# Two gated matmul stages behind windowed attention: the sign bit of float64 weight words travels through ScalarE instead of VectorE

## The chip, the cores and the metric

The kernel runs on one core of a Trainium2 chip. The metric is the device time of one execution in microseconds, the median of several runs. The core has five engines with an instruction queue each, which run in order and meet only through semaphores: TensorE (PE, with its weight loads as PEld), VectorE (DVE), ScalarE (ACT), GpSimd (POOL) and SyncE (SP), which issues most of the DMAs.

## The reference

Attention over 4 batches, 8 heads, 576 positions and a head width of 64, with a causal window of 128 and a bias that falls with distance. Its output (2304 tokens of 512 values) goes through two dense stages:

```python
h = np.maximum(np.maximum(x @ w1, x @ w2), x @ w3)     # 512 -> 768
x = (h @ w_out).astype(np.float32)                     # 768 -> 512
g, val = x @ w_gate, x @ w_val                         # 512 -> 1536
out = (g / (1.0 + np.exp(-g)) * val) @ w_out           # 1536 -> 512
```

The weights arrive as float64, since they are float32 numbers that were multiplied by a float64 scalar. q, k, v are float32.

## The kernel before

Every matmul of float32 precision is made of three with operands of lower precision: an operand is kept as a head (its rounded value) and a rest (what rounding took away), and head times head, head times rest and rest times head are summed in PSUM.

The work is laid out as one program of pieces that are interleaved by hand. The attention is cut into units of up to 128 queries of one pair of heads; each unit passes through scores, normalising, transposes and values (`st_scores`, `st_normalise`, `st_transpose`, `st_values`). The first dense stage (`up_groups`, `down_groups`) runs between these units as soon as tokens are there, over six chunks of 384 tokens. The second dense stage (`second`) begins near 434 us in the profile; it uses seven products per block in place of eight, so it needs sums of weight blocks (`mixed`, line 582) and sums of token blocks (`token_sum`, line 646), and it walks over 12 blocks of hidden columns (`STEPS`). `spread` and the loop over `STEPS` say which piece is written behind which; the order that each engine then gets is chosen by a planner, which lays the instructions out in time by its own estimates of their costs and prefers the pieces under `high_priority`.

The change lies in `single` (lines 113 to 126), which turns float64 words into float32 in place. A weight tile lies in SBUF as pairs of 32-bit words, `lo` and `hi`. Line 118 (ACT) reads `hi` as a float32 and multiplies it by 2^-112, which takes 896 from the 11-bit exponent of the float64; the result goes into `w`, a tile of which there is one buffer (`wconv`). Line 121 (DVE) shifts `w` left by three bits, so that exponent and mantissa lie where a float32 has them; the sign, in bit 31, falls out. Line 122 (DVE) takes the sign from `hi` and puts it into `w`. Line 124 (DVE) shifts `lo` right by 29, which gives the last three mantissa bits, joins them with `w` and writes the finished float32 over `lo`.

`single` is called once for a tile by `prep_up` (9 tiles of 128 x 1024 for the first dense stage), `prep_down` (12 of 128 x 256), and `gates`, `values` and `outs` (36 of 128 x 512 for the second): 57 calls. What follows a call is `split`: line 129 (ACT) rounds the float32 to the head, and `low` (line 107, on DVE or POOL) subtracts to get the rest. The next call's line 118 can't write `w` before line 124 of the last call has read it.

Other lines that the prediction names: 359, 365 and 370 work on the scores (DVE, DVE, ACT's Exp); 380 and 387 are reciprocal and scaling on DVE; 398 is PE's transpose, 410 ACT's copy of its result; 201 is the maximum in the first dense stage; 621 loads token blocks (`yr`); 681 to 683 are PE's products in the second dense stage and 704 is ACT's copy of the first of them (`s`); 718 and 733 are Silu on ACT.

Of the kernel before, what the change touches and what calls it, by code (L numbers as in the profile page):

```python
# [8 lines left out]
F32 = mybir.dt.float32  # L9
# [3 lines left out]
AF = mybir.ActivationFunctionType  # L13
ALU = mybir.AluOpType
# [57 lines left out]
def kernel(ctx: ExitStack, tc, *args):  # L72
    n = len(NATIVE)
    qs, ks, qks = (dict(zip(u, x)) for u, x in ((NATIVE, args), (NATIVE, args[n:]), (ORDER[n:], args[2 * n:])))
    vv, w123, wo1, wgv, wo2, out = args[-6:]
# [10 lines left out]
    nc = tc.nc  # L86
# [26 lines left out]
    def single(raw, pinned=False):  # L113

        n = raw.shape[1]
        lo, hi = raw[:, :, 0], raw[:, :, 1]
        w = wconv.tile([P, 1024], I32, tag="wf", name="wf")[:, :n]
        first = nc.scalar.activation(out=w.bitcast(F32), in_=hi.bitcast(F32), func=AF.Copy, scale=2.0 ** -112)  # L118
        if pinned:
            tc.keep_in_program_order(first)  # L120
        nc.vector.tensor_scalar(out=w, in0=w, scalar1=3, scalar2=None, op0=ALU.logical_shift_left)
        nc.vector.scalar_tensor_tensor(out=w, in0=hi, scalar=-0x80000000, in1=w,
                                       op0=ALU.bitwise_and, op1=ALU.bitwise_or)
        nc.vector.scalar_tensor_tensor(out=lo, in0=lo, scalar=29, in1=w,  # L124
                                       op0=ALU.logical_shift_right, op1=ALU.bitwise_or)
        return lo.bitcast(F32)
# [5 lines left out]
    def prep_w(raw, t, pinned=False, rest=nc.vector):  # L132
        split(t, single(raw, pinned), rest)
# [118 lines left out]
    first = {}  # L252
# [300 lines left out]
    def second(apool, raws2, ps_o):  # L553
# [5 lines left out]
        def prep(f):  # L559
# [8 lines left out]
            def gates():  # L568
                ab[0] = single(raw[0])
                t[0] = up_tile(f"u{f}_0")  # L570
                split(t[0], ab[0], nc.vector)

            def values():
                ab[1] = single(raw[1])
                both = up_tile(f"u{f}_3") if f % 2 == 0 else ws[f - 1][5]
                t[3], t[5] = both[:, :, f % 2 * 256:f % 2 * 256 + 256], both
                split(t[3], ab[1][:, 256:], nc.vector)
# [368 lines left out]
```

## Time and profile before

| what | value |
|---|---|
| median of 3 runs | 849.52 us (849.43 to 849.52) |
| time of the profiled execution | 849.52 us |
| its span, first to last instruction | 847.8 us |
| granted clock of TensorE, mean of the span | 0.998 |
| PE busy | 834.7 us, 98% of the span |
| DVE busy | 599.0 us, 71% |
| ACT busy | 423.3 us, 50% |
| POOL busy | 382.9 us, 45% |

The span is the time from the first instruction of the program to the last one's end; the time of an execution holds 1.72 us more. Busy time of PE comes from matmuls that overlap, with modelled ends: a PE that is busy throughout may still be waiting a little between matmuls. In the views below, "idle" before an instruction is time in which its engine did nothing, and behind the arrow stands what ended the wait.

### The profile page before, as it was taken

The numbers are of one execution on the slowest core, as the hardware profiler recorded it, in microseconds if no ns is written. First come the engines' busy times: TensorE is split into PE (matmuls) and PEld (weight loads), VectorE is DVE, ScalarE is ACT, GpSimd is POOL, SyncE is SP. The second block draws the span as 40 slices with busy tenths as digits, with TensorE's granted clock in tenths as the row PEclk, the third lists the DMA queues.
The fourth block names the chain that finished last, engine by engine and source line by source line (L and its number), as shares of the span: only waits on it lengthen the run. The fifth ranks groups of instructions, "written<-read, shape, count | busy, mean of one in ns | idle before, by whom it ended". The sixth has DMA issues, their size and how long they took to land.

```text
span 847.8 us, 14703 instructions
## 1 busy us (share of the span) xinstructions
PE 834.7 (98%) x4760; PEld 781.0 (92%) x4760; DVE 599.0 (71%) x1593; ACT 423.3 (50%) x1146; POOL 382.9 (45%) x551
## 2 busy tenths in 40 slices
PE   8899999999999999999999999999999999999998
PEld 6589898999999999999999999999999999999996
DVE  8999798877666877549979999994753854343442
ACT  6776786776666677425356555553312422212220
POOL 2768898578877568635314232212311211211110
PEclk9999999999999999999999999999999999999999
DMA  9754443343232232314447498724947412827322
GB/s 328 250 168 147 123 130 112 122 137 95 81 113 92 65 117 62 108 37 147 145 163 281 162 342 300 250 87 145 352 148 262 147 65 77 299 98 253 106 75 99
DMA packets 62780, 133.34 MB, mean 157 GB/s; under 512 B 6768, under 2 KB 24176, under 8 KB 61552
## 3 DMA queue, kind: packets, MB, share of 16 engines
q1 hardware_dynamic: 59248, 127.69, 44.4%
q10 hardware_dynamic: 3456, 4.72, 1.6%
q8 instruction: 37, 0.61, 0.3%
q14 instruction: 39, 0.32, 0.1%
HBM read 96.99 MB, written 35.39 MB: 156 GB/s over the span
## 4 chain that ended last, share of the span: by engine, by line
PE 86%; DVE 7%; issue 2%; DMA 2%; POOL 1%; ACT 1%; SPq 0%; DVEq 0%; POOLq 0%; ACTq 0%
PE ps L157 9%; PE ps L156 9%; PE ps L158 9%; PE pg L682 7%; PE pg L681 7%; PE pg L683 7%; PE po L763 6%; PE po L762 6%; PE po L761 6%; PE pc L683 3%; PE pc L682 3%; PE pc L681 3%; PE pv L445 2%; PE sc L350 2%; PE pt L398 2%
## 5 line engine op out<-in xcount | busy, mean ns | idle before, releaser
L107 POOL TENSOR_TENSOR act<-h,act 128x384 fp32r<-128x384 f32 x72 | 79.6, 1126 | 287.4 <-ACT act L129 242.7
L157 PE MATMUL ps<-x,w 128*128 128x384 f32 x432 | 147.2, 341 | 0.0
L156 PE MATMUL ps<-x,w 128*128 128x384 f32 x432 | 146.0, 343 | 0.9 <-ACT m L199 0.9
L158 PE MATMUL ps<-x,w 128*128 128x384 f32 x432 | 146.3, 339 | 0.0
L681 PE MATMUL pg<-ya,u 128*128 128x384 f32 x360 | 120.4, 335 | 1.7 <-ACT s L704 1.7
L682 PE MATMUL pg<-ya,u 128*128 128x384 f32 x360 | 121.0, 336 | 0.0
L683 PE MATMUL pg<-ya,u 128*128 128x384 f32 x360 | 120.4, 335 | 0.0
L762 PE MATMUL po<-u,act 128*128 128x512 f32 x216 | 85.2, 394 | 0.0
L763 PE MATMUL po<-u,act 128*128 128x512 f32 x216 | 85.1, 395 | 0.0
L414 POOL TENSOR_SCALAR_AFFINE_SELECT t<-pk 128x512 fp32r<-128x512 f32 (+2 forms) x128 | 73.3, 595 | 24.2 <-DVE pk L107 16.1
L761 PE MATMUL po<-u,act 128*128 128x512 f32 x216 | 83.9, 389 | 0.0
L156 PEld LDWEIGHTS ps<-x,w 128*128 128x128 f32 x432 | 80.8, 188 | 2.7 <-ACT m L199 1.2
L690 DVE TENSOR_TENSOR u<-pg,s 128x384 f32<-128x384 f32 x72 | 39.7, 552 | 60.8 <-PE pg L683 60.6
L157 PEld LDWEIGHTS ps<-x,w 128*128 128x128 f32 x432 | 81.2, 188 | 1.3 <-issue 0.7
L158 PEld LDWEIGHTS ps<-x,w 128*128 128x128 f32 x432 | 81.2, 188 | 0.7 <-issue 0.7
L681 PEld LDWEIGHTS pg<-ya,u 128*128 128x128 f32 x360 | 67.6, 188 | 5.8 <-ACT s L704 2.0
L682 PEld LDWEIGHTS pg<-ya,u 128*128 128x128 f32 x360 | 67.6, 188 | 4.6
L370 ACT ACTIVATE z<-z,mn 128x128 f32<-128x128 f32 (+1 forms) x160 | 63.2, 398 | 10.5 <-DVE mn L365 10.1
L683 PEld LDWEIGHTS pg<-ya,u 128*128 128x128 f32 x360 | 67.6, 188 | 0.5
L718 ACT ACTIVATE h<-s 128x384 f32<-128x384 f32 x36 | 18.9, 524 | 90.7 <-DVE s L690 90.6
L118 ACT ACTIVATE wf<-wr 128x512 f32<-128x512 f32 (+2 forms) x57 | 39.8, 698 | 31.4 <-DVE wr L124 14.6
L690 DVE TENSOR_TENSOR u<-pc,u 128x384 f32<-128x384 f32 x72 | 39.8, 553 | 17.4 <-PE pc L683 17.1
(122 smaller groups left out, 2065.2 us busy)
## 6 DMA issues: line engine op xcount, KB each, us to landing
ya<-a_dram SPq DMA_DIRECT2D x56, 384.0 KB, 4.8
a_dram<-ya SPq DMA_DIRECT2D x42, 384.0 KB, 5.2
wr<-wgv SPq DMA_DIRECT2D x24, 512.0 KB, 4.5
wr<-w SPq DMA_DIRECT2D x9, 1024.0 KB, 5.5
qkr<-qk SPq DMA_DIRECT2D x32, 288.0 KB, 2.9
o_dram<-acc SPq DMA_DIRECT2D x36, 256.0 KB, 3.0
acc<-o_dram SPq DMA_DIRECT2D x36, 256.0 KB, 2.7
wr<-wo SPq DMA_DIRECT2D x12, 512.0 KB, 4.9
```

The costliest lines, as they stand in the source:

```text
L107: eng.tensor_tensor(out=out, in0=raw, in1=head.bitcast(F32), op=ALU.subtract)
L156: nc.tensor.matmul(ps, wh, xt_h, start=first, stop=False)
L157: nc.tensor.matmul(ps, wh, xt_l, start=False, stop=False)
L158: nc.tensor.matmul(ps, wl, xt_h, start=False, stop=last)
L414: nc.gpsimd.affine_select(out=t[:, i, :n, :, :m], in_=w[:, :n, :, :m], compare_op=op, fill=0.0, base=0, pattern=[[0, n], [0, 2], [-sign, m ...
L681: nc.tensor.matmul(o, wh, y[:, 0], start=first and k == 0, stop=False, skip_group_check=True)
L682: nc.tensor.matmul(o, wh, y[:, 1], start=False, stop=False, skip_group_check=True)
L683: nc.tensor.matmul(o, wl, y[:, 0], start=False, stop=k == 1, skip_group_check=True)
L690: nc.vector.tensor_tensor(out=o, in0=x, in1=y, op=ALU.add)
L761: nc.tensor.matmul(po, ah, w[:, 0], start=j == 0, stop=False)
L762: nc.tensor.matmul(po, ah, w[:, 1], start=False, stop=False)
L763: nc.tensor.matmul(po, al, w[:, 0], start=False, stop=j == PASS - 1)
```

## The change

Line 118 calls the parametric ReLU in place of Copy, with the same scale and a slope of 2^32 for negative inputs. A positive word is scaled as before. A negative one is multiplied by 2^32 as well, which adds 32 to its 8-bit exponent field and so sets bit 28, which is zero otherwise. Line 121 shifts by three, and bit 28 becomes bit 31, the sign. Line 122 is gone. Lines 121 and 124 stay as they were (124 becomes 122).

```diff
-        first = nc.scalar.activation(out=w.bitcast(F32), in_=hi.bitcast(F32), func=AF.Copy, scale=2.0 ** -112)
+        first = nc.scalar.activation(out=w.bitcast(F32), in_=hi.bitcast(F32), func=AF.Prelu, scale=2.0 ** -112, alpha=2.0 ** 32)
         if pinned:
             tc.keep_in_program_order(first)
         nc.vector.tensor_scalar(out=w, in0=w, scalar1=3, scalar2=None, op0=ALU.logical_shift_left)
-        nc.vector.scalar_tensor_tensor(out=w, in0=hi, scalar=-0x80000000, in1=w,
-                                       op0=ALU.bitwise_and, op1=ALU.bitwise_or)
         nc.vector.scalar_tensor_tensor(out=lo, in0=lo, scalar=29, in1=w,
                                        op0=ALU.logical_shift_right, op1=ALU.bitwise_or)
         return lo.bitcast(F32)
```

## Rows read from the trace of the kernel before

**Rows 1.** The page: busy time of each engine, share of the span, instructions.

```profile
PE 834.7 (98%) x4760; PEld 781.0 (92%) x4760; DVE 599.0 (71%) x1593; ACT 423.3 (50%) x1146; POOL 382.9 (45%) x551
```

**Rows 2.** Stretches: length, busy PE, PEld, DVE, ACT, POOL; clock, DMA share, GB/s.

```profile
0.00:20.00 20.00, 17.35 (x102) 12.75 (x102) 16.02 (x91) 12.29 (x44) 5.20 (x18) 1.00 0.90 326
20.00:40.00 20.00, 16.33 (x104) 11.84 (x100) 19.47 (x71) 14.84 (x50) 13.34 (x21) 0.91 0.73 245
...
100.00:120.00 20.00, 19.06 (x121) 18.12 (x120) 18.27 (x67) 16.87 (x55) 18.67 (x26) 1.00 0.47 145
...
420.00:440.00 20.00, 18.31 (x106) 17.99 (x105) 16.17 (x27) 9.76 (x18) 5.13 (x4) 1.00 0.67 234
...
500.00:520.00 20.00, 20.00 (x107) 18.73 (x106) 18.90 (x37) 11.36 (x25) 6.07 (x5) 1.00 0.81 279
840.00:848.00 8.00, 4.13 (x19) 3.08 (x17) 2.14 (x4) 0.00 (x0) 0.00 (x0) 1.00 0.51 189
```

**Rows 3.** PE's waits: for whom; us in total, times, the longest.

```profile
PE pg L681 <- ACT s L704: 1.7, 1, 1.7
PE pt L398 <- DVE z L387: 1.5, 1, 1.5
```

**Rows 4.** The removed instruction by form, on DVE, the form of 128 x 512.

```profile
L122 DVE SCALAR_TENSOR_TENSOR wf<-wr,wf 128x512 int32<-128x512 int32 x36 | 28.8, 799 | 0.4
```

**Rows 5.** Line 122 alone by stretch: length, busy DVE and count; clock, DMA, GB/s.

```profile
0.00:45.00 45.00, 4.89 (x4) 0.96 0.79 279
45.00:145.00 100.00, 14.20 (x17) 1.00 0.45 141
...
385.00:440.00 55.00, 6.70 (x9) 1.00 0.49 169
440.00:700.00 260.00, 21.39 (x26) 1.00 0.59 208
```

**Rows 6.** DVE in order of time near 25 us: start, duration, instruction.

```profile
23.52 1.24 DVE L122 SCALAR_TENSOR_TENSOR wf<-wr,wf 128x1024 int32<-128x1024 int32 x1
...
25.47 1.36 DVE L124 SCALAR_TENSOR_TENSOR wr<-wr,wf 128x1024 int32<-128x1024 int32 x1
...
26.83 0.35 DVE L387 TENSOR_SCALAR z<-z,rc 128x128 f32<-128x128 f32 x1
```

**Rows 7.** Stretches of 4 us near the first stalls, columns as in rows 2.

```profile
24.00:28.00 4.00, 2.27 (x24) 1.32 (x20) 4.00 (x16) 2.04 (x5) 2.46 (x4) 1.00 0.86 312
28.00:32.00 4.00, 4.00 (x23) 2.77 (x19) 4.00 (x13) 3.36 (x12) 2.00 (x3) 0.60 0.11 36
...
36.00:40.00 4.00, 2.98 (x21) 2.24 (x20) 3.98 (x15) 2.33 (x8) 3.35 (x5) 1.00 0.63 182
```

**Rows 8.** The chain that ended last, from 427 us: start, duration, what.

```profile
427.33 4.89 DMA yr<-y_dram
432.32 1.73 DVE yr L646
434.05 0.60 DVE wf L122
...
435.59 0.61 DVE wr L124
436.22 0.66 ACT u L129
436.89 0.38 ACT s L704
```

**Rows 9.** ACT by form: busy us, mean ns; idle before and its releaser.

```profile
L370 ACT ACTIVATE z<-z,mn 128x128 f32<-128x128 f32 x128 | 50.6, 398 | 9.1 <-DVE mn L365 8.9
L129 ACT CAST act<-h 128x384 fp32r<-128x384 f32 x72 | 33.5, 512 | 32.9 <-DVE h L693 32.9
...
L718 ACT ACTIVATE h<-s 128x384 f32<-128x384 f32 x36 | 18.9, 524 | 90.7 <-DVE s L690 90.6
...
L434 ACT CAST x<-pv 128x128 fp32r<-128x128 f32 x24 | 6.3, 261 | 6.7 <-PE pv L428 6.7
...
L733 ACT ACT_TABLE_LOAD x1 | 1.3, 1283 | 1.1 <-PE pg L683 1.1
```

## The prediction

> **What bounds the kernel now.** I read the busy times of the page first. PE is busy for 834.7 us of a span of 847.8 us [rows 1], so the whole kernel can gain 13.1 us at most by filling PE's idle time, whatever DVE is spared. The next question is where those 13.1 us lie, and the table of stretches answers it [rows 2]. At the end, from 840 us, 3.87 us are idle (8.00 less 4.13): the last addition and the last store, with no weight conversion near. The idle time that lies beside conversions is 2.65 us in the first 20 us, 3.67 us in the next 20, 0.94 us from 100 to 120, and 1.69 us from 420 to 440: 8.95 us together. In the stretch from 20 to 40 the granted clock is 0.91 as well, which is a loss of 0.09 x 20 = 1.8 us that the busy time hides. So 8.95 + 1.8 = 10.75 us is the most that the change can reach through PE.
>
> The third view is who ends PE's waits [rows 3]. Its longest wait, 1.7 us, is for ACT's copy at line 704 at the entry to the second dense stage; the next, 1.5 us, is for line 387 on DVE. DVE is 19.47 us of 20 busy from 20 to 40 us, 18.27 of 20 from 100 to 120 [rows 2]. There DVE is a second bound beside PE, and a shorter DVE queue can be worth something. From 500 to 520 us DVE is nearly as full (18.90 of 20), yet PE is busy for 20.00 of 20: there, what DVE is spared is worth nothing.
>
> **What is removed.** Line 122 costs 799 ns in its commonest form [rows 4], 57 of them in all. By stretch [rows 5]: 4 of them with 4.89 us in the first 45 us, 17 with 14.20 us up to 145 us, 9 with 6.70 us from 385 to 440, 26 with 21.39 us from 440 to 700; one more lies between. The 26 late ones, 45% of the sum, lie under a PE that has no idle time, so I cost their removal at nothing; what hides it is the products of the second dense stage. If that cover were gone (DVE late for PE), they would be worth up to 21.39 us, but no row there shows PE waiting.
>
> The first stall. At 23.52 us a line 122 takes 1.24 us on DVE; line 124 follows at 25.47 for 1.36 us, and behind it line 387 at 26.83 makes the operand of the transpose for which PE has been idle for 1.48 us (the 1.5 us wait) [rows 3, 6]. DVE has no gap in that stretch (4.00 of 4.00 busy [rows 7]). The removed 1.24 us stands in the same queue ahead of line 387, and another of its size stands some 8 us earlier (the four early ones average 4.89 / 4 = 1.22 us [rows 5]). Two of them are 2.46 us, more than the 1.48 us of the wait. So I take the wait as gone: 1.5 us. What is late next is ACT or POOL work of the neighbouring attention units; the bounds are 0 (another wait takes its place) and 3.67 us (all the idle time of the stretch).
>
> The clock behind it. In the 4 us with that stall PE is busy for 2.27 us, and in the next 4 us the granted clock is 0.60, a part of them at the lower level, 1.2 GHz in place of 2.4. From 36 to 40 us PE is busy for 2.98 us, and the rows show 1.00 there [rows 7]. With 1.48 us of the gap gone, the stretch from 24 to 28 would have 2.27 + 1.48 = 3.75 us busy, more than the one that kept its clock. So I take the fall of the clock as gone too: 0.40 x 4 = 1.6 us. Bounds: 0 and 1.8 us, and below nothing if a stall moves to where it brings the clock down once more (1.6 us lost).
>
> The entry to the second dense stage. The chain there goes from a load of a token block at 427.33 (4.89 us) through additions on DVE, a line 122 at 434.05 (0.60 us), line 124, ACT's line 129 and ACT's line 704, for which PE waits 1.7 us [rows 3, 8]. That load waits on SP for a weight buffer to come free, and the buffer comes free from DVE's work on the conversions. Of the 9 removed instructions between 385 and 440 us, 8 lie ahead of the load or in it and one behind it, at 0.6 to 0.8 us each [rows 4, 5, 8]; even three of them would cover 1.7 us. The loads of later weights on SP's queue come earlier by the same. I take 1.6 us of the 1.69 us that PE idles in the stretch [rows 2]. Bounds: 0 and 1.69.
>
> The stretch from 45 to 145 us holds the largest number of removed instructions (17) but little idle time, 0.94 us from 100 to 120 [rows 2]; a load lies ahead of that gap as well. I take 0.3 us; bounds 0 and 0.94.
>
> **What is added.** Line 118 changes its function, not its size. No row shows a parametric ReLU. The nearest one is Silu over 128 x 384 at 524 ns against 512 ns for a cast of the same shape: 12 ns more [rows 9]. The far one is Exp, with a bias read from SBUF and a sum, over 128 x 128 at 398 ns against 261 ns for a cast: 137 ns more [rows 9]. I take the near one, since scale and slope are plain numbers as they are for Silu: 57 x 12 ns = 0.7 us, spread over ACT, which is half idle [rows 1]. The far end is 57 x 137 ns = 7.8 us of ACT, some 21/57 of it (2.9 us) in the stretch where attention waits for ACT too; a tenth of that reaching PE would be 0.3 us. In the sum it is nothing. The Trainium skill, page "ScalarE: Activation LUTs", section "What ACT_TABLE_LOAD costs", adds about 93 ns for each operand that an ACTIVATE reads by pointer; by it the estimate would be 57 x 93 ns = 5.3 us of ACT at most, and the row for Silu, 524 ns, shows no such addition.
>
> What else moves: no DMA is added. No wait is added: line 121 waits for line 118 as before, and line 124 now follows it directly. The next line 118 gets the one `w` buffer earlier. The planner, however, lays out every queue anew with 57 instructions fewer, and this is the cost that no row gives. I take 0, and as its bounds one stall like the first, with its clock, to either side: 1.5 + 1.6 = 3.1 us.
>
> **The sum.** 1.5 + 1.6 + 1.6 + 0.3 = 5.0 us. The profiled execution took 849.52 us, 1.72 us more than its span, and is itself the median of the runs shown. 849.5 - 5.0 = 844.5 us.
>
> **The rivals.** First: only the entry to the second stage gains, because the early stalls belong to the attention's own chain of ACT, POOL and DVE, which is late by another link when one is shortened. For it: several of PE's early waits are ended by ACT and POOL. Against it: DVE without a gap. Time: 849.5 - 1.7 = 847.8 us, on the border of what can be told from no change (0.2% is 1.7 us, about what a measurement of this kernel can tell; below I use that bound).
>
> Second: nothing is gained, because the planner fills the room with earlier conversions, and the load at 427 us waits for something else: 849.5 us.
>
> Third, the other side: conversions move forward in ACT's queue. In the first 45 us ACT works on line 118 and line 129 in turn with the Exp and the copies that feed transposes; both work on 128 x 1024. If the planner, with a shorter DVE part per conversion, puts line 129 of a conversion ahead of such a copy and it must wait there for line 124, the copy waits with it. It decides from the point where that wait is longer than PE's queued work; then one more stall with its clock comes, 3.1 us, and nothing is regained: 852.6 us. For it: ACT is only 14.84 us of 20 busy there and waits in order. Against it: line 124 now comes sooner.
>
> Fourth, a table: ACT might have to load a table for the new function between Exp and Silu. The trace has a load before Silu, 1283 ns [rows 9]. 21 conversions lie among Exp in the first 145 us, with two loads each 21 x 2 x 1.283 = 54 us. ACT's three early rows average 14.7 us of 20 [rows 2], so some 145 x 0.267 = 39 us are free, and 15 us at least go over: 865 us or more. The Trainium skill, page "ScalarE: Activation LUTs", section "Table sets: the hidden batching unit", says that cheap functions such as relu and copy stand in every set; it doesn't name the parametric one there, and no run here shows it. One load serves Exp and Copy in this trace, which speaks for cheap functions being shared.
>
> **How the numbers follow.** My forecast, a gain of 3 to 8 us: 0.50. A larger gain, up to the bound of 10.75 us: 0.05. First rival 0.17, half of it beyond the border (0.09) and half within (0.08). Second 0.11. Third 0.13. Fourth 0.04. So faster 0.50 + 0.05 + 0.09 = 0.64, same 0.08 + 0.11 = 0.19, slower 0.17. The range goes from 840.0 (the forecast and nearly all of the larger gain) to 851.5 (the two rivals near no change and the nearer third of the third): about 0.15 is left out, the fourth, most of the third and a little of the large gains.
>
> **What would show it.** Right: PE's idle time from 20 to 40 us falls from 3.67 us to near 2, the clock row near 28 us reads 1.00, PE's wait for line 704 is gone, the last 8 us are as before, DVE's busy time falls by about 48 us, and line 118 keeps its duration within 20 ns. Wrong: the clock falls elsewhere in the first 45 us; the wait at the entry to the second stage stands with a load as its releaser; more table loads than now; or PE's waits on ACT's copies grow.

## The result and the profile after

The changed kernel takes 853.1 us (852.67 to 858.31, 6 runs), the kernel before 849.61 us (849.43 to 849.91, 6 runs) beside it. The ratio of the times, after over before, is 1.0051 with a 95% interval of 1.0028 to 1.0074: it is slower by 0.5% (0.4% by the medians; one run of after took 858.31 us, at a mean granted clock of 0.992). The forecast was 844.5 us and its range ended at 851.5, so it was wrong in sign and in range. The profiled execution of after took 853.82 us, with a span of 852.1 and a mean granted clock of 0.996. Behind the old line 122 all line numbers of after are smaller by two (704 is 702, 129 is 127, 124 is 122).

The page, busy time of each engine, to be read beside [rows 1]:

```profile
PE 836.6 (98%) x4760; PEld 781.8 (92%) x4760; DVE 556.9 (65%) x1536; ACT 423.7 (50%) x1146; POOL 364.6 (43%) x551
```

DVE lost its 57 instructions and 42.1 us. ACT is as busy as before. PE has two microseconds more busy time, and the table of stretches tells where from; the columns are those of [rows 2].

```profile
0.00:20.00 20.00, 17.04 (x98) 12.63 (x98) 15.56 (x89) 12.27 (x40) 5.88 (x18) 1.00 0.91 327
20.00:40.00 20.00, 16.78 (x110) 12.02 (x109) 19.14 (x73) 16.72 (x57) 12.66 (x21) 1.00 0.84 284
100.00:120.00 20.00, 19.38 (x119) 17.39 (x118) 16.27 (x62) 15.46 (x53) 17.85 (x28) 1.00 0.35 108
420.00:440.00 20.00, 19.78 (x113) 19.14 (x112) 7.59 (x11) 8.29 (x15) 6.31 (x5) 1.00 0.27 86
440.00:460.00 20.00, 18.77 (x105) 18.00 (x105) 15.41 (x28) 10.78 (x23) 6.82 (x6) 1.00 0.77 285
460.00:480.00 20.00, 16.68 (x86) 15.55 (x85) 18.37 (x36) 9.78 (x21) 4.82 (x4) 0.91 0.60 190
480.00:500.00 20.00, 20.00 (x96) 18.41 (x95) 12.30 (x22) 9.27 (x20) 7.01 (x6) 0.92 0.65 236
```

Idle time of PE is 20 less its busy time, and (1 - clock) x 20 is the PE time that the lower clock takes. In these seven stretches:

| stretch, us | idle before | idle after | clock before | clock after |
|---|---|---|---|---|
| 0 to 20 | 2.65 | 2.96 | 0 | 0 |
| 20 to 40 | 3.67 | 3.22 | 1.8 | 0 |
| 100 to 120 | 0.94 | 0.62 | 0 | 0 |
| 420 to 440 | 1.69 | 0.22 | 0 | 0 |
| 440 to 460 | 0 | 1.23 | 0 | 0 |
| 460 to 480 | 0 | 3.32 | 0 | 1.8 |
| 480 to 500 | 0 | 0 | 0 | 1.6 |
| sum | 8.95 | 11.57 | 1.8 | 3.4 |

The sums are 10.75 before (the 8.95 + 1.8 of the prediction) and 14.97 after. Their difference of 4.2 us is close to the 4.3 us by which the span grew (852.1 - 847.8). The three stretches up to 120 us gave 2.3 us back (1.8 of it the clock), the one from 420 to 440 us gave 1.5, and the second dense stage from 440 us, where PE had been busy throughout, took away 7.95. PE's waits by their enders (us in total, times, longest) name the large one:

```profile
PE po L759 <- ACT act L127: 3.3, 1, 3.3
PE pt L396 <- ACT pk L408: 1.6, 3, 1.2
...
PE pg L679 <- ACT s L702: 1.2, 1, 1.2
```

The 1.7 us for the first copies by line 704 of [rows 3], at the entry to the second stage, are gone. The 1.2 us for line 702 are a new wait, for a later copy, and it ends at 445.89 us. ACT in order of time ahead of that copy (start, duration, and in brackets the idle time before and its ender):

```profile
438.53 0.49 ACT L731 ACTIVATE h<-pg 128x384 f32<-128x384 f32 x1
444.26 0.66 ACT L118 ACTIVATE wf<-wr 128x512 f32<-128x512 f32 x1 [5.24 <-DMA wr<-wo]
444.82 0.51 ACT L716 ACTIVATE h<-s 128x384 f32<-128x384 f32 x1
445.36 0.48 ACT L702 COPY s<-pg 128x384 f32<-128x384 f32 x1
```

A line 118 stood still for 5.24 us, until its block of down weights (`wo`) had landed, and the Silu and the copy behind it in the queue waited with it. The 3.3 us for `act` are new as well. ACT around them, in the same columns:

```profile
471.41 0.93 ACT L127 CAST ya<-yr 128x384 fp32r<-128x384 f32 x2 [0.85 <-DMA yr<-y_dram]
476.62 0.66 ACT L118 ACTIVATE wf<-wr 128x512 f32<-128x512 f32 x1 [4.28 <-DMA wr<-wo]
477.18 0.91 ACT L127 CAST act<-h 128x384 fp32r<-128x384 f32 x2
```

And the chain that ended last, over the same time:

```profile
470.06 6.54 DMA wr<-wo
476.60 0.02 issue
476.62 0.03 ACT wf L118
476.65 0.53 issue
477.18 0.51 ACT act L127
477.69 0.04 issue
477.73 0.80 PE po L759
```

Here too ACT stood still, for 4.28 us, at a line 118 whose block of down weights was still under way, and behind it in the same queue stood the two casts whose result PE needed. The clock fell to its lower level, 1.2 GHz, at 476.5 us, in that gap, and stayed there for 6.8 us: half of that, 3.4 us, is the clock's column of the table. In four of the other five runs of after the mean clock was 0.997 or 0.998, so they lost less to the clock than the profiled one (0.996).

In the order of ACT's queue this line 118 stands directly ahead of those casts. In the kernel before the same line 118 stands behind six instructions that it precedes here: both casts, two Silu and two copies. There it waits for its load too:

```profile
484.56 0.67 ACT L118 ACTIVATE wf<-wr 128x512 f32<-128x512 f32 x1 [2.80 <-DMA wr<-wo]
```

That load was issued at 479.19 us, 9 us later than the 470.06 us of after, and yet PE was busy for 20.00 of 20 us from 480 to 500 us. So it is not a later load that makes the stall of after; what is new is the work that stands behind the wait.

### The profile page after: what moved, and what is told of

Read it like the earlier page. It is cut to its first block, busy times and chain, and to the rows that moved or that the text cites. A ratio compares the mean times of both kernels' runs of the same rounds, so it can differ in the third digit from the quotient of the medians.

```text
span 852.1 us, 14597 instructions
## 1 busy us (share of the span) xinstructions
PE 836.6 (98%) x4760; PEld 781.8 (92%) x4760; DVE 556.9 (65%) x1536; ACT 423.7 (50%) x1146; POOL 364.6 (43%) x551
## 5 line engine op out<-in xcount | busy, mean ns | idle before, releaser
L107 POOL TENSOR_TENSOR act<-h,act 128x384 fp32r<-128x384 f32 x72 | 77.6, 1099 | 293.8 <-ACT act L127 237.5
L118 ACT ACTIVATE wf<-wr 128x512 f32<-128x512 f32 (+2 forms) x57 | 39.7, 696 | 32.0 <-DMA wr<-wo 23.7
L702 ACT COPY s<-pg 128x384 f32<-128x384 f32 x36 | 17.3, 480 | 75.9 <-PE pg L681 75.8
```

The source lines that it names most:

```text
L107: eng.tensor_tensor(out=out, in0=raw, in1=head.bitcast(F32), op=ALU.subtract)
```

## The experiments

Ratios below are time over the time of the kernel before on the same chip (849.9 to 850.2 us), with 95% intervals. Differences in us between two kernels that ran beside different measurements of the kernel before hold up to 0.6 us of theirs (849.61 to 850.24). The theory that arose from the profile is that the removal itself gains and the planner's new order loses, in the second stage through the place of that one line 118. The rivals are that the new function costs something, that the loss belongs to the removal in any order, that the load is what is late, and that the stall matters less than the clock early in the kernel.

**The function alone.** Line 118 with the parametric ReLU, line 122 kept; every queue has the order of before.

```diff
-        first = nc.scalar.activation(..., func=AF.Copy, scale=2.0 ** -112)
+        first = nc.scalar.activation(..., func=AF.Prelu, scale=2.0 ** -112, alpha=2.0 ** 32)
...
         nc.vector.scalar_tensor_tensor(out=w, in0=hi, scalar=-0x80000000, in1=w,
                                        op0=ALU.bitwise_and, op1=ALU.bitwise_or)
```

> Line 118 calls the parametric ReLU as in the changed kernel, but line 122 of the kernel before stays (it sets a sign that is set already), and every engine's queue has the order of the kernel before. Theory (the loss is one of order, the function costs nothing): 849.6 us, within 0.5, line 118 at 670 ns within 5, two table loads of 1283 ns. Rival (the function itself costs): some 0.14 us for each of 57, 850.5 to 853 us, and line 118 longer.

It took 849.9 us, ratio 1.0002 (0.9993 to 1.0011). ACT by form in after (busy us, mean ns of one, idle before), the new function at 128 x 512 and both table loads:

```profile
L118 ACT ACTIVATE wf<-wr 128x512 f32<-128x512 f32 x36 | 24.1, 669 | 23.9 <-DMA wr<-wo 15.8 <-DVE wr L122 4.3 <-DMA wr<-wgv 3.3
...
L368 ACT ACT_TABLE_LOAD x1 | 1.3, 1283 | 0.8 <-PEq L933 0.8
L731 ACT ACT_TABLE_LOAD x1 | 1.3, 1283 | 0.0
```

Copy took 671 ns at this shape in the kernel before, which had two table loads of 1283 ns as well. The new function costs nothing.

**The removal alone.** The code of after, with each engine held to the order that it had before, less line 122. A recorded list per engine gives the order, and neighbours in it are tied without a wait:

```diff
         tile_attention_moe_moe_kernel(tc, *args)
+        keep_orders(nc, tc)   # per engine: for a, b in zip(order, order[1:]):
+                              #   tc.add_manual_dep(mine[b], mine[a].name, DependencyInfo(NoSync, DATA))
```

> The changed kernel, but each queue is held in the order that it has in the kernel before, with line 122 left out. Theory (the removal itself is worth what the forecast's sum said, and the new order takes it away): 844.5 to 846 us, PE's wait of 1.5 us near 27 us and its wait of 1.7 us near 435 us gone. Rival (PE is the bound everywhere and the removal is worth nothing): 849.5 us. Rival (without line 122 something in the second stage is late whatever the order): 852 us or more.

It took 846.68 us (845.04 to 847.28, 5 runs, all with a clock of 1.000), ratio 0.9954 (0.9942 to 0.9966). Stretches, and PE's waits, of this kernel, in its fastest run:

```profile
0.00:20.00 20.00, 16.60 (x96) 12.26 (x97) 14.78 (x89) 11.54 (x44) 6.22 (x18) 1.00 0.92 323
20.00:40.00 20.00, 16.88 (x114) 12.12 (x112) 16.99 (x70) 16.19 (x54) 11.36 (x21) 1.00 0.77 262
...
420.00:440.00 20.00, 19.32 (x112) 19.00 (x111) 12.32 (x21) 9.49 (x18) 3.17 (x2) 1.00 0.47 155
440.00:460.00 20.00, 20.00 (x114) 19.61 (x113) 18.49 (x33) 12.89 (x28) 8.43 (x7) 1.00 0.82 296
460.00:480.00 20.00, 20.00 (x108) 18.82 (x107) 19.12 (x34) 11.00 (x23) 4.57 (x5) 1.00 0.49 153
```

```profile
PE pt L396 <- ACT pk L408: 2.2, 5, 1.0
PE pv L426 <- POOL t L412: 1.6, 4, 0.9
...
PE pg L679 <- ACT s L702: 0.7, 1, 0.7
```

The removal gains 3.3 us (849.99 - 846.68), and the second stage keeps its cover: 20.00 of 20. So the loss is the order's: 853.1 - 846.7 = 6.4 us. The waits also show where it stayed below the forecast's 5.0. The clock from 20 to 40 us is 1.00, as forecast, and the entry wait fell from 1.7 to 0.7. But the first stall didn't vanish: PE now waits for ACT's copies (line 408) and POOL's selections (line 412).

**The order alone.** Line 122 kept, directly behind line 121, with all else in the order of after.

```diff
         nc.vector.tensor_scalar(out=w, in0=w, scalar1=3, scalar2=None, op0=ALU.logical_shift_left)
+        nc.vector.scalar_tensor_tensor(out=w, in0=hi, scalar=-0x80000000, in1=w,
+                                       op0=ALU.bitwise_and, op1=ALU.bitwise_or)
```

> The kernel before, with line 122 in place, but each queue is held in the order that it has in the changed kernel (line 122 directly behind its line 121). Theory (the order is what costs): 853 us or more, with PE's long wait near 474 us for ACT's line 129 and a fall of the clock behind it; up to some 6 us more than the changed kernel, since the early stalls are back. Rival (the removal is what costs): near 849.5 us.

It took 877.19 us, ratio 1.0316 (1.0302 to 1.0329). PE's waits:

```profile
PE po L761 <- ACT act L129: 5.6, 2, 5.2
PE ps L156 <- DVE m L201: 4.4, 3, 1.6
PE pv L428 <- POOL t L414: 3.5, 6, 1.7
```

The same wait for `act` heads the list, now with 5.2 us at once. Up to some 6 us more than after had been expected. The loss isn't in one place: PE's idle time is larger than in after by 4.3 us up to 45 us, by 5.7 from 45 to 145, by 4.2 from 385 to 440 and by 4.1 from 440 to 520. With this order line 122 is worth 877.2 - 853.1 = 24 us, in the order of before 3.3 us. The two parts of the change are not a sum: an order laid out for a DVE without line 122 is far worse with it than the old order was. What an instruction is worth depends on the order into which it is put.

**One instruction moved.** The orders of after, except that the stalled line 118 goes two places back in ACT's queue, behind the two casts.

```diff
-    ACT: [..., 118 of wo, 127 act<-h, 127 act<-h, ...]
+    ACT: [..., 127 act<-h, 127 act<-h, 118 of wo, ...]
```

> The changed kernel in its own orders, but for one instruction: the line 118 of the conversion that waits at 476.6 us for its weights stands two places later in ACT's queue, behind the two casts for which PE waits 3.3 us. Theory (this one place makes the wait and the fall of the clock): the 3.3 us wait and some 3.4 us at half clock are gone, 846 to 847.5 us. Rival (DVE, which also waits there for line 118, makes PE wait in the same place): a wait of 2 us or more near 476 us stays, 850 to 853 us. Rival (the late load only moves its wait to the next copy on ACT): 849 to 851 us.

It took 849.8 us (847.19 to 853.14, 12 runs), ratio 0.9996 (0.9983 to 1.001), 3.3 us less than after. ACT in order of time:

```profile
473.40 0.93 ACT L127 CAST act<-h 128x384 fp32r<-128x384 f32 x2 [1.44 <-DVE h L691]
476.68 0.68 ACT L118 ACTIVATE wf<-wr 128x512 f32<-128x512 f32 x1 [2.35 <-DMA wr<-wo]
```

The load lands at the same time as in after, so line 118 starts at the same time (476.68 us against 476.62), and the casts are done 3.8 us earlier. PE's gap there fell from 3.3 to 0.1 us, as the theory had it, but the time stayed above its 846 to 847.5 us. The runs spread more than the stall explains: those with a mean clock of 0.999 or 1.000 took 847.2 to 849.3 us, those with 0.995 to 0.998 took 850.3 to 853.1.

**The whole conversion moved.** The same conversion moved further: its line 118 six places back, its lines 121 and 122 on DVE seven places back.

```diff
-    ACT: [..., 118 of wo, <6 others>, ...]    DVE: [..., 121, 122 of wo, <7 others>, ...]
+    ACT: [..., <6 others>, 118 of wo, ...]    DVE: [..., <7 others>, 121, 122 of wo, ...]
```

> The changed kernel in its own orders, but for the three instructions of that one conversion: line 118 goes six places back on ACT (to where it stands in the kernel before, behind two casts, two Silu and two copies), lines 121 and 122 go seven places back on DVE, behind the additions that had queued behind them. Theory (the early place in both queues is what costs, and what is left when only ACT's is mended is DVE's part and the landing of the load): 846.5 to 848 us, with the single runs within 2 us of one another. Rival (another place of the new order loses as much, whatever is done here): 849 to 851 us and as wide as when one was moved.

It took 850.67 us (846.32 to 852.09, 12 runs), ratio 0.9998 (0.9985 to 1.0011). Moving it further gains nothing more, and the spread stayed: 4 runs at a mean clock of 0.999 or 1.000 took 846.3 to 848.4 us, 8 at 0.996 took 850.4 to 852.1. So the spread is not this conversion's, and the runs were not within 2 us of one another as the theory had it. It follows the clock, which falls in some runs and not in others; the two halves of the order, further below, put most of that into the early part.

**The planner, told to leave them.** `single` can keep line 118 in written order; here for the down weights of the second stage, with the planner laying out the rest anew.

```diff
-                ab[2] = single(raw[2])
+                ab[2] = single(raw[2], pinned=True)
```

> The changed kernel, planned anew with one instruction held: line 118 of a conversion of down weights may not stand on ACT ahead of what is written before it. Theory (the planner puts it forward because it takes the load as landed): PE's wait of 3.3 us for line 127's casts is gone, no fall of the clock near 476 us, 846 to 849 us. Rival (the plan finds another stall of the size): 850 to 853 us.

It took 849.17 us (844.96 to 851.0), ratio 0.9976 (0.9963 to 0.999). In its profile the longest wait of PE between 400 and 840 us is 0.19 us. The three runs with a clock of 1.000 took 845.0 to 846.5 us, the two with 0.998 took 848.4 and 849.0, the seven with 0.995 or 0.996 took 849.2 to 851.0; in the profiled one the clock fell at 23.7 us, for 3.4 us. The second stage is whole; the start is not.

**An earlier load.** The loads of the first four blocks of down weights written one conversion earlier, planned anew: if the load is what is late, this mends it.

```diff
-                return out + [piece for pieces in todo for piece in pieces[4:]]
+                loads, outs = [pieces[4] for pieces in todo], [pieces[5] for pieces in todo]
+                return out + loads[:1] + [piece for n in range(len(todo)) for piece in loads[n + 1:n + 2] + outs[n:n + 1]]
```

> The changed kernel, planned anew, with the load of each of the first four down weights written one conversion earlier. Theory (the load that lands late is what ACT waits for): the wait on ACT for that load falls from 4.3 us to near 0, 846 to 849 us. Rival (the load waits on SP for one of five buffers, so that writing it earlier only holds up the loads behind it): 851 us or more.

It took 851.3 us (848.39 to 856.23), ratio 1.0017 (1.0001 to 1.0032). PE's wait for `act`, and the load ahead of it in the chain:

```profile
PE po L760 <- ACT act L127: 1.5, 1, 1.5
```

```profile
471.18 4.91 DMA wr<-wo
```

Line 118 still waits 21.0 us in 11 waits for `wr<-wo` (23.7 us in 11 in after). Written earlier, the load was not issued earlier: 471.18 us against 470.06 in after. So the outcome is the rival's, and what a load that is really earlier would be worth, this run doesn't show. The place of line 118 can be mended in the order of ACT, the load's time could not be in this way.

**A sliver of line 122.** After, with line 122 on 8 of its columns, so that the planner lays out a third order.

```diff
+        nc.vector.scalar_tensor_tensor(out=w[:, :8], in0=hi[:, :8], scalar=-0x80000000, in1=w[:, :8],
+                                       op0=ALU.bitwise_and, op1=ALU.bitwise_or)
```

> The changed kernel with line 122 of the kernel before kept on 8 columns only (it sets a sign that is set already): some 57 x 0.1 us on DVE in place of 47.9 us. Planned anew. Theory (each plan finds its own stalls, and the time of one says little of the next): off the changed kernel's 853.1 us by 2 us or more, to either side, from 844 to 858 us, with stalls in other places. Rival (the time follows the work on DVE): within 1 us of the changed kernel, 852 to 854 us.

It took 849.49 us (847.88 to 852.59), ratio 0.9993 (0.9981 to 1.0004): with 57 instructions more than after it is 3.6 us faster. Its largest stalls lie elsewhere (near 21, 26, 129 and 439 us); the longest:

```profile
PE pg L681 <- ACT h L733: 1.5, 1, 1.5
```

Between after and this kernel the time doesn't follow DVE's work, it follows the order.

**The two halves of the order.** The order of before up to some 365 us and that of after behind it, and the reverse.

```diff
-    order of after, whole
+    e9_old_head: before's order to 365 us, after's order behind
+    e10_old_tail: after's order to 365 us, before's order behind
```

> The changed kernel with each queue held to the order of the kernel before up to some 365 us (line 122 left out), and to its own order behind that. Theory (the second stage's order is most of the loss): 849.5 to 852 us, the wait of 3.3 us near 474 us and the fall of the clock behind it as in the changed kernel, and the early stretch as when the removal stands alone. Rival (the early order is the loss): 846 to 847.5 us.

> The other half: the changed kernel's own order up to some 365 us, the order of the kernel before behind that. Theory (the early order costs nothing in the mean): 846 to 847.5 us, the clock whole. Rival (the new early order has a stall of 1.4 us near 21 us, behind which the clock falls in part of the runs): 848 to 850.5 us, with single runs in two groups some 3.4 us apart by their mean clock (1.000 and 0.996).

With the old head it took 852.82 us (851.58 to 853.44), ratio 1.0033 (1.0021 to 1.0045). The wait for `act` and the two stretches around it:

```profile
PE po L759 <- ACT act L127: 4.3, 1, 4.3
```

```profile
460.00:480.00 20.00, 15.72 (x81) 14.68 (x80) 17.40 (x34) 8.81 (x19) 4.81 (x4) 0.94 0.58 183
480.00:500.00 20.00, 20.00 (x102) 18.44 (x101) 12.62 (x22) 9.28 (x20) 7.05 (x6) 0.97 0.69 252
```

With the old tail it took 848.77 us (846.57 to 854.23, 12 runs), ratio 0.9987 (0.9973 to 1.0001), in two groups: six runs with a clock of 0.999 or 1.000 at 846.6 to 847.6 us, six with 0.993 to 0.996 at 849.9 to 854.2; that is the rival's outcome. Against the removal alone, the new order behind 365 us costs 852.8 - 846.7 = 6.1 us by the medians, with its five runs within 1.9 us of one another, and the new order ahead of it 848.8 - 846.7 = 2.1 us, which is about nothing in the six runs whose clock held. The profiled run of the old tail, 854.23 us, shows where it doesn't:

```profile
20.00:24.00 4.00, 2.45 (x14) 1.33 (x12) 3.98 (x10) 3.35 (x14) 1.98 (x2) 1.00 0.95 305
24.00:28.00 4.00, 3.60 (x15) 2.44 (x16) 2.02 (x12) 3.05 (x7) 1.42 (x4) 0.51 0.91 325
```

The same two stretches in the profiled run of after, which has that order at this place:

```profile
20.00:24.00 4.00, 2.07 (x12) 1.03 (x12) 3.99 (x17) 3.35 (x14) 2.00 (x4) 1.00 0.80 243
24.00:28.00 4.00, 3.77 (x26) 2.80 (x26) 3.22 (x10) 3.38 (x12) 0.90 (x3) 1.00 0.99 306
```

PE was idle for longer in after (1.93 us of 4 against 1.55), yet kept its clock; in the old tail it didn't. Not all of the 854.23 us is the early order's: the clock of this run fell once more, from 440 to 460 us (0.91, 1.8 us), behind a wait of 2.0 us at the entry to the second stage, in the old order.

**One place, against the old head.** The old head as above, with the one line 118 two places back.

```diff
-    ACT: [..., 118 of wo, 127 act<-h, 127 act<-h, ...]
+    ACT: [..., 127 act<-h, 127 act<-h, 118 of wo, ...]
```

> As the kernel with the old head (old order up to some 365 us, the changed kernel's own behind that; 852.82 us), but for the one line 118 that goes two places back on ACT, behind the two casts. The early stretch, which makes the clock differ from run to run in the new early order, is out of it. Theory (that one place is all that the second stage loses): 846.5 to 848 us, the wait of some 4 us near 474 us below 0.5, no fall of the clock behind it. Rival (the rest of the new second-stage order loses as well): 849 to 851 us.

It took 847.93 us (846.4 to 849.53, 8 runs, all with a clock of 0.999 or 1.000), ratio 0.9976 (0.9965 to 0.9986).

```profile
460.00:480.00 20.00, 19.34 (x103) 17.68 (x102) 17.35 (x34) 9.58 (x21) 4.68 (x4) 1.00 0.58 184
480.00:500.00 20.00, 20.00 (x103) 18.15 (x103) 14.93 (x28) 11.55 (x26) 6.54 (x5) 1.00 0.80 285
```

852.82 - 847.93 = 4.9 us for one instruction in one queue, two places from where it was. The stretches say about the same: PE's idle time there falls from 4.28 to 0.66 us (3.6), and the clock's loss from (0.06 + 0.03) x 20 = 1.8 us to nothing, 5.4 us together; the profiled run, 849.53 us, is the slowest of the eight, and its span is only 3.5 us shorter. What is left in the second stage is the other wait seen in after: 1.0 us of PE for line 702, behind a line 118 that waits 5.03 us for its load.

**The version that beats both.** The order of before up to some 365 us, and behind it the order that the planner gave with the pinned conversions.

```diff
-    order of after, whole
+    before's order to 365 us, the pinned kernel's order behind
```

> The order of the kernel before up to some 365 us, and behind that the order that the planner gave with line 118 of the down weights held in the written order; line 122 is out. The best of both as far as known. Theory (the early stretch then keeps its clock and the second stage has no stall over 0.4 us): 845 to 846.5 us, faster than the removal alone by some 0.5 us. Rival (the stalls seen with the pin come from the stretch near 464 us and take the clock): 847.5 to 849.5 us.

It took 845.09 us (844.82 to 845.78, 5 runs), ratio 0.9946 (0.9934 to 0.9958), at a clock of 0.999 or 1.000 in every run. Both waits behind a line 118 are gone:

```profile
440.00:460.00 20.00, 20.00 (x113) 19.48 (x112) 18.79 (x30) 12.65 (x28) 8.02 (x7) 1.00 0.64 236
460.00:480.00 20.00, 19.83 (x105) 18.26 (x104) 19.93 (x37) 11.55 (x24) 6.94 (x6) 1.00 0.68 239
```

It is the fastest measured, though its interval overlaps that of the removal alone.

## Why the prediction was wrong

**The step that failed** is the sentence on the planner: "I take 0, and as its bounds one stall like the first, with its clock, to either side: 1.5 + 1.6 = 3.1 us." It measured 6.4 us on the bad side, twice the bound. 6.1 us were measured for the new order behind 365 us alone, and 4.9 of these hang on the place of one instruction. The term was sized by the first stall, one of those in the trace of before. A new order can put a stall where the old one had none, and there it was larger: 3.3 us in after and 4.3 in the old head's, with a clock fall that took 3.4 and 1.8 us in these profiled runs.

**"The 26 late ones ... I cost their removal at nothing"** was right for the removal: held to the old order, PE stays busy for 20.00 of 20 from 440 to 480 us. But the working then asked only whether DVE could be late for PE there. It was ACT's queue in its new order that took the cover away. That nothing in a covered stretch can gain doesn't mean that nothing in it can lose.

**The third rival** had the mechanism: a conversion moves forward in ACT's queue and holds up work behind it. Its price of 852.6 us is near the 853.1 by luck: it is one early stall of 3.1 us with nothing regained, and the runs show 3.3 us regained and 6.4 lost. Its place was wrong, the first 45 us for the second stage, and so was what is waited for, line 124 for a load. It got a chance of 0.13. The rows for a better one were at hand: line 118 already waited for loads of weights in the trace of before (8.1 us for `wr<-wo` in 6 waits), in a queue that holds the casts for PE.

**The terms of the sum.** The first wait, 1.5 us: mis-sized. The wait for line 387 went, and ACT's copies and POOL's selections came in its place, as the bound of 0 had it. In the removal alone the idle time from 20 to 40 us fell by 0.55 us (3.67 to 3.12), and that from 0 to 20 rose by 0.75 (2.65 to 3.40). The entry, 1.6 us: 1.0 in the removal alone (1.69 to 0.68). The stretch from 100 to 120 us, 0.3 us: right (0.94 to 0.64).

The clock near 28 us, 1.6 us: right that the fall goes, 1.00 in after's profile and in the removal alone. But the reasoning behind it (a stretch busier than that of [rows 7] from 36 us keeps its clock) was too sure, since gaps of nearly the same size near 21 us bring the clock down in some runs only. And its price is in doubt. Beside the experiments the kernel before ran 87 times: 43 runs had a mean clock of 0.999 or 1.000 and a median of 850.1 us, and 39 had 0.997 or 0.998, as the profiled one had, and a median of 849.9. In that kernel a run that kept its clock was no faster. In the two profiles the four stretches of the prediction give the removal 1.1 us of idle time and 1.8 us of clock; the 87 runs say that the 1.8 can't be taken as a gain by itself. No trace shows a run of the kernel before that kept its clock, so how the 3.3 us divide stays open.

**The function** was right at nothing: 669 ns against 671 of Copy, and two table loads as before. The fourth rival is out. The Trainium skill, page "ScalarE: Activation LUTs", section "Table sets: the hidden batching unit", left open whether the parametric form stands in every set; here it shares Exp's and Silu's. By the price for operands in the section "What ACT_TABLE_LOAD costs" of that page, quoted in the prediction, which is one for an operand read by pointer, 57 instructions would have cost an estimated 5.3 us of ACT; the rows show none of it for a scale and slope given as plain numbers.

**The signs that were named.** Line 118 kept its duration within 20 ns: seen. DVE's busy time fell by 42.1 us, not 48: other instructions of DVE grew by the rest. The idle time from 20 to 40 us fell to 3.22 us, not to 2. The clock near 28 us reads 1.00: seen. The last 8 us are as before: seen, PE busy for 4.33 us against 4.13. The wait for line 704 at the entry is gone: seen, but a new one of 1.2 us ends some 9 us further on, and its releaser stood behind a line 118 that waited for a load. Of the signs for wrong, "PE's waits on ACT's copies grow" is the one that came: from 1.0 to 1.6 us for line 408 (410 before), and from nothing to 3.3 us for the casts of `act`.

**What stays open.** Why a gap near 21 us takes the clock in one run and not in the next. What a load that is issued earlier would be worth. Why the load at 470.06 took 6.54 us, when loads of this kind take 4.7 us in the median of the page: SP issued five stores right behind it, which may have shared the DMA engines with it, but no run varied that. And why the planner chose that place; its own estimates of time are in no trace.

## What to carry to other kernels

Where a planner or scheduler lays out the queues, an edit has two prices, its work and the new order, and the second can be the larger: measure the edit once with the old order held, and only then with the new one. In an in-order queue look for instructions that wait for a DMA and ask which work stands behind them; put such an instruction behind the casts that TensorE needs, or pin it. A stretch with a full TensorE promises no gain, but it must stand in the list of what can be lost.

## What the runs showed of the hardware

The clock was seen to fall to its lower level for 3.4 us (the old head, near 478 us) or 6.8 us (after, from 476.5 us), behind gaps of PE. The mean clock of one and the same kernel differed from run to run: the old tail had 0.999 or 1.000 in six of twelve runs, and its median then depends on how often the clock falls, 846.6 to 847.6 us against 849.9 to 854.2. That isn't so in every kernel: in the kernel before, runs with 0.999 or 1.000 and runs with 0.997 or 0.998 took the same (850.1 and 849.9 us). An in-order queue passes on a wait for a DMA: 5.24 us of ACT behind one line 118 became 1.2 us of PE, 4.28 us behind another 3.3 us. The parametric ReLU, with scale and slope as plain numbers, costs on ACT what Copy costs (669 and 671 ns at 128 x 512), with a slope as large as 2^32.
